# Attention plus two expert layers on one core: order of weight loads and splits, width of the filler's products, and which engine makes the first unit's sums

## The chip, the cores and the metric

The kernel runs on one core of one Trainium2 chip. The metric is the device time of one execution in microseconds (us). The median of three runs before the change is 2114.24 us, from 2111.54 to 2114.75. The trace that is read here is of a fourth execution, the profiled one, which took 2118.01 us; its span from the first to the last instruction is 2116.2 us.

## The reference

Three layers follow one another, all in float32.

```python
# 1. attention: 4 batches x 8 heads, 512 local and 32 global tokens, head size 64, window 32
out_g = softmax(q_g @ [k_g, k_l]^T / 8) @ [v_g, v_l]
out_l = softmax([q_l @ k_g^T / 8, masked(q_l @ k_l^T / 8)]) @ [v_g, v_l]
x = rows of both, 2176 x 512
# 2. eight experts, mixed by Sinkhorn weights
P = exp(x @ w_gate - max)
8 times: P /= P.sum(1); P /= P.sum(0); P *= N / E
x = sum over e of P[:, e] * (relu(x @ w1[e]) @ w2[e])        # 512 -> 1024 -> 512
# 3. one wide layer
x = elu(x @ w_in) @ w_out                                    # 512 -> 2048 -> 512
```

The weights of the last layer come as float64 and are made into float32 pairs by the kernel.

## The kernel before

Every float32 operand of a large product is kept as a rounded high part ("h") and a rest ("l"), and a product is three matmuls, hh, hl and lh (`three`, L107 to L114; L853 to L855). The high part is a cast on ScalarE (ACT), the rest a subtraction on VectorE (DVE) or GpSimd (POOL). All DMAs go through the one queue of SyncE (SP). Each engine works its own instructions off in the order of the program, which is written out by hand (`manual_schedule`).

The stages, with the times of the profiled execution:

- **Attention, about 0 to 262 us** (L470 to L590). TensorE gets filler between the pieces of attention: `filler` (L460) runs half-experts 0 and 1 ("units" u) on the 1024 tokens of the first part by `unit_plain` (L413). That one treats a block of 512 tokens as two halves of 256 columns: four PSUM tiles of the first product (`mm1`), each of 12 matmuls of 256 columns, then two tiles of the second product (`mm2_part`) of 12 matmuls of 512 columns each. Every matmul is one step of the generator; `fill_for(200)` takes steps worth about 200 ns. `swap` loads and splits unit 1's weights beside it, at counted steps.
- **Transition, about 262 to 350 us** (L941 to L959). What is left of the filler runs as a loop. Every 4th step takes one entry of `pre`, every 8th one of `plan`. `pre` holds the sums of blocks of x (`sums_of_x`, L617: `whole` adds high and rest, `comb` adds or subtracts two blocks, `hi` and `lo` split the result), two loads, and the start of unit 2's weights (`weights1`, L663). `plan` is the Sinkhorn iteration (`sinkhorn`, L760): `rows` on DVE, then a matmul (`pcs`, L794) that waits for `rows`, then `cols` on DVE. What is left of `plan` is laid between the products of the first unit.
- **Units on the first part of the tokens (p = 0), units 2 to 15, about 303 to 884 us, and on the second part (p = 1), units 0 to 15, about 884 to 1728 us** (loop at L960). A unit is `mix1` and then `mix2_all`. `mix1` makes the first product in a seven-product scheme: 13 products of six matmuls of 512 columns for p = 0, 27 products of six matmuls of 288 columns for p = 1. Each product ends in PSUM and is taken out by ACT (s, L834) and DVE (u, L836; t, L822); ACT then makes hh (L825) from t, and DVE the rest hl (L827) from t and hh. There are eight PSUM banks and three buffers of t. After each product one entry of the list `side1` is issued. `mix2_all` makes eight or nine second products of twelve matmuls of 512 columns; after each, four entries of `side2` are issued.
- **The wide layer, about 1728 us to the end** (L1043 on), which the change doesn't touch.

What stands in the two lists before the change: `side1` is the four splits of this unit's second weights (`nbuild`; `split`, L99: cast L101 on ACT, subtraction L105 on POOL), then the two loads of the next unit's first weights (`ld1`, L669), then the loads of float64 pieces (L728). `side2` is the building of the next unit's first weights (`b1`, 18 entries), then the conversion of one or two float64 pieces (`weights64`, L720: `words` is six DVE instructions, `parts` two ACT and three POOL instructions and two stores to scratch, L755 and L756, each waiting on SP for what it stores), then the two loads of the next unit's second weights (`ld2`, L714). Raw weights, float64 pieces and block sums share four buffers (`raw_tile`). Units 20 to 25 of the list `order`, counted from 0, convert two pieces, the other units one; the first two and the last before the change of part convert none.

Of the kernel before, what the change touches and what calls it, by code (L numbers as in the profile page):

```python
# [16 lines left out]
ALU = mybir.AluOpType  # L17
# [31 lines left out]
def tile_net(ctx: ExitStack, tc, kq, vw, vc, qg, wg, w1, w2, wi, wo, consts, out):  # L49
# [362 lines left out]

    def unit_plain(u, b, swap=None):  # L413

        for c0 in (0, 256):
            leave, come = (swap is not None and u == v and c0 == 256 * (1 - v) for v in (0, 1))
            hh, hl = (hs[p][:, :, c0:c0 + 256] for p in "hl")
            if leave:
                next(swap)
                next(swap)  # L420
            n = 0
            for r in mm1(wA, lambda p, k: xcols(p, k, b)[:, c0:c0 + 256], 256, hh, hl):
                yield r
                n += 1
                if come and n % 12 == 0:
                    next(swap, None)
            n = 0
            for o in (0, 128):
                i = b * 4 + (c0 + o) // 128
                ps = psm.tile([128, 512], F32, tag="m", name="m2")  # L430
                for r in mm2_part(wA, ps, hh, hl, o, range(4)):
                    yield r
                    n += 1
                    if leave and n % 6 == 0:
                        next(swap)
                if u == 0:
                    nc.vector.tensor_copy(accs[i], ps)
                else:
                    nc.vector.tensor_tensor(out=accs[i], in0=ps, in1=accs[i], op=ALU.add)
                yield "q"  # L440

    rawp = att.enter_context(tc.tile_pool(name="rawp", bufs=3, side="left"))

# [173 lines left out]
    def sums_of_x(p, m):  # L617

        v = {}

        def blk(n, q):
            return xop[n + q][:, :, :m]

        def whole(n, src, eng):
            v[n] = raw_tile((2, m), F32, "x" + n)
            eng.tensor_tensor(out=v[n], in0=blk(src, "h").bitcast(F32), in1=blk(src, "l").bitcast(F32), op=ALU.add)

        def comb(dst, a, b, op, buf):
            nc.vector.tensor_tensor(out=v[buf], in0=v[a], in1=v[b], op=op)
            v[dst] = v[buf]  # L630

        def hi(n):
            nc.scalar.copy(blk(n, "h"), v[n])

        def lo(n):
            nc.vector.tensor_tensor(out=blk(n, "l"), in0=v[n], in1=blk(n, "h").bitcast(F32), op=ALU.subtract)

        load = [
            lambda n=n, q=q, k=k, i=i: nc.sync.dma_start(
                xop[n + q][:, :, :m].bitcast(F32), xd[q][:, 2 * k:2 * k + 2, i * m:(i + 1) * m]  # L640
            )
            for n, i, k in (("s4", 1, 0), ("22", 1, 1), ("11", 0, 0), ("12", 0, 1)) for q in "hl"
        ] if p else []
        return load, [
            lambda: whole("21", "s4", nc.gpsimd),
            lambda: whole("22", "22", nc.vector),
            lambda: comb("s1", "21", "22", ALU.add, "22"),
            lambda: hi("s1"),
            lambda: whole("11", "11", nc.gpsimd),
            lambda: lo("s1"),  # L650
            lambda: comb("s3", "11", "21", ALU.subtract, "21"),
            lambda: comb("s2", "s1", "11", ALU.subtract, "22"),
            lambda: hi("s2"),
            lambda: hi("s3"),
            lambda: lo("s2"),
            lambda: lo("s3"),
            lambda: whole("12", "12", nc.vector),
            lambda: comb("s4", "12", "s2", ALU.subtract, "12"),
            lambda: hi("s4"),
            lambda: lo("s4"),  # L660
        ]

    def weights1(u):  # L663

        v = {}

# [15 lines left out]

        def lo(n):
            src = v[n] if n[0] == "t" else blk(n)
            nc.vector.tensor_tensor(out=wop[n + "l"], in0=src, in1=wop[n + "h"].bitcast(F32), op=ALU.subtract)  # L685

        g, sub = nc.gpsimd, ALU.subtract
        return [lambda: load(0), lambda: load(1)], [
# [71 lines left out]
    def sinkhorn():  # L760
# [31 lines left out]
        def cols():  # L792
            ps = ps2.tile([128, 512], F32, tag="n", name="pcs")
            nc.tensor.matmul(ps[:, :E], ones, s["c"], start=True, stop=True)  # L794
            r = sm.tile([128, E], F32, tag="rc", name="rc")
            nc.vector.tensor_scalar_add(r, ps[:, :E], 1e-9)
            nc.vector.reciprocal(r, r)
            nc.vector.tensor_tensor(
                out=pr, in0=pr, in1=r.rearrange("p (o e) -> p o e", o=1).to_broadcast([128, NT, E]), op=ALU.mult
            )  # L800
            nc.vector.tensor_scalar_mul(pr, pr, float(T) / E)

        return [gmax, None, expm] + [rows, None, cols] * 8

# [136 lines left out]
    with tc.manual_schedule():  # L941
        conv = deque(range(8 * U2))
        plan, sums = sinkhorn(), sums_of_x(0, SL)[1]
        first, build = weights1(2)

        pre, plan = deque(sums[:-2] + first + build[:9]), deque(plan)
        steps = 0
        for r in fill:
            steps += 1
            if steps % 4 == 0:  # L950
                pop(pre)
            if steps % 8 == 0:
                pop(plan)
        pop(pre, len(pre))
        for f in build[9:13]:
# [4 lines left out]
        for a, (p, u) in enumerate(order):  # L960
            after = order[a + 1] if a + 1 < len(order) else None
            switch = after is not None and after[0] != p
            if a > 0:
                side1.extendleft(reversed(nbuild))
            else:
                side1.extend(nbuild)
            cv = []
            if after is not None:
                ld1, b1 = weights1(after[1])
                ld2, nbuild = weights2(after[1])  # L970
                side1.extend(ld1)
                if not switch:
                    for _ in range(min(len(conv), 0 if a < 2 else 2 if 19 < a < 26 else 1)):
                        cv.append(weights64(conv.popleft()))
                    side1.extend(ld for ld, _ in cv)
            if a == 0:

                rest, n = list(side1), len(plan)
                side1.clear()
                for b in range(n):  # L980
                    side1.extend(rest[b * len(rest) // n:(b + 1) * len(rest) // n])
                    side1.append(plan.popleft())
            last = mix1(p, u)
            pop(side1, len(side1))
            if after is None:
                break
            if switch:
                ldx, sums = sums_of_x(1, HALF)

                for f in ldx[4:]:  # L990
                    f()
                b1 = ldx[:4] + [f for pair in zip(b1, sums[:12]) for f in pair] + b1[12:] + sums[12:14]
                nbuild = sums[14:] + nbuild
            side2.extend(b1)
            for _, ops in cv:
                side2.extend(ops)
            side2.extend(ld2)
            mix2_all(p, u, last)
            pop(side2, len(side2))
            if switch:  # L1000
                for i in range(TP[0] // 128):
                    nc.sync.dma_start(yd[:, i], accs[i])
# [176 lines left out]
```

## Time and profile before

| what | value |
|---|---|
| median of three runs | 2114.24 us |
| the three runs | 2114.24, 2114.75, 2111.54 us |
| profiled execution: its time, its span | 2118.01 us, 2116.2 us |
| mean granted TensorE clock | 0.979 |
| busy share of the span: PE, PEld, DVE, ACT, POOL | 96, 84, 64, 35, 34 % |

PE is TensorE with its matmuls, PEld the loading of weights into it. Matmuls are pipelined, so a busy PE is not a PE at its peak; its idle time is real. In timelines the first number is the start of an instruction in us from the start of the span, the second its length, x2 says that two like it follow one another, and in brackets stand the idle time of the engine ahead of it and what ended that. In rows of windows the columns are the stretch, its length, busy time of PE, PEld, DVE, ACT and POOL (with the count of instructions), the granted clock of TensorE as a share of full speed, the busy share of the DMA engines and their GB/s.

### The profile page before, as it was taken

What the parts mean: (1) busy time and instruction counts of PE and PEld (TensorE: products, weight loads), DVE (VectorE), ACT (ScalarE), POOL (GpSimd) and SP (SyncE); (2) the same over time, 40 slices, a digit from 0 to 9 for tenths busy, and PEclk for the clock granted to TensorE, in tenths of its full rate; (3) what the DMA queues carried; (4) which work ended last, traced back from release to release, by engine and by line L of the source; (5) the groups of instructions that cost most, each with busy time, mean ns of one, the idle gap of its engine ahead of it and who ended that gap; (6) DMA issues with size and microseconds to landing.
All of it is one profiled execution on the core that took longest, in us unless ns stands there. A gap on an engine that the chain in (4) does not pass through costs nothing.

```text
span 2116.2 us, 29201 instructions
## 1 busy us (share of the span) xinstructions
PE 2026.4 (96%) x11115; PEld 1768.1 (84%) x11115; DVE 1362.9 (64%) x2534; ACT 747.0 (35%) x1488; POOL 710.1 (34%) x605
## 2 busy tenths in 40 slices
PE   9999979999999999899999988888999999999999
PEld 8998968888888888788888877787888888888897
DVE  7666586676776776766666666666666654444454
ACT  6555424323333332233333322222233333343343
POOL 6545313233333433323322233333332211222222
PEclk9999999999999999999999999999999999999999
DMA  7435221123112211422211222222221140202001
GB/s 229 136 121 175 70 91 60 30 65 114 61 60 97 83 60 68 149 100 82 70 61 60 71 80 80 79 71 71 70 76 64 51 179 1 80 1 80 1 31 55
DMA packets 56444, 168.45 MB, mean 80 GB/s; under 512 B 6128, under 2 KB 7920, under 8 KB 54256
## 3 DMA queue, kind: packets, MB, share of 16 engines
q1 hardware_dynamic: 56304, 166.59, 23.5%
q8 instruction: 87, 1.43, 0.3%
q14 instruction: 53, 0.43, 0.1%
HBM read 138.52 MB, written 28.05 MB: 79 GB/s over the span
## 4 chain that ended last, share of the span: by engine, by line
PE 73%; DVE 10%; ACT 5%; issue 5%; DMA 4%; POOL 2%; SPq 0%; DVEq 0%; ACTq 0%; POOLq 0%
PE m L113 13%; PE m L109 13%; PE m L111 13%; PE q L853 8%; PE q L855 7%; PE q L854 7%; DMA w2r<-in_w_dram 3%; PE o L310 2%; DVE hl L827 2%; DVE eg L130 2%; PE m L1088 1%; PE m L1087 1%; PE m L1090 1%; ACT w2h L101 1%; PE ptp L293 1%
## 5 line engine op out<-in xcount | busy, mean ns | idle before, releaser
L113 PE MATMUL m<-w2h,hl 128*128 128x512 f32 x1088 | 427.0, 392 | 0.0
L109 PE MATMUL m<-w2h,hh 128*128 128x512 f32 x1088 | 426.9, 392 | 0.0
L111 PE MATMUL m<-w2l,hh 128*128 128x512 f32 x1088 | 426.9, 392 | 0.0
L827 DVE SCALAR_TENSOR_TENSOR hl<-t,hh 128x288 fp32r<-128x288 f32 (+1 forms) x368 | 262.9, 714 | 108.5 <-ACT hh L825 103.6
L825 ACT ACTIVATE hh<-t 128x288 fp32r<-128x288 f32 (+1 forms) x368 | 182.1, 500 | 347.8 <-DVE t L822 347.8
L891 DVE SCALAR_TENSOR_TENSOR acc<-m,pr,acc 128x512 f32<-128x512 f32 x247 | 184.3, 749 | 179.6 <-PE m L113 177.9
L105 POOL TENSOR_TENSOR w2l<-w2r,w2h 128x512 fp32r<-128x512 f32 x120 | 171.3, 1457 | 202.2 <-ACT w2h L101 202.2
L113 PEld LDWEIGHTS m<-w2h,hl 128*128 128x128 f32 x1088 | 204.3, 188 | 41.4
L111 PEld LDWEIGHTS m<-w2l,hh 128*128 128x128 f32 x1088 | 204.4, 188 | 40.6
L109 PEld LDWEIGHTS m<-w2h,hh 128*128 128x128 f32 x1088 | 204.4, 188 | 40.1
L822 DVE TENSOR_TENSOR t<-q,u 128x288 f32<-128x288 f32 (+1 forms) x276 | 144.9, 525 | 62.2 <-PE q L855 55.1
L677 POOL TENSOR_TENSOR wt<-w1r 128x512 f32<-128x512 f32 x60 | 78.6, 1311 | 300.1 <-DVE hl L827 251.0
L130 DVE SCALAR_TENSOR_TENSOR eg<-eg,er 128x384 f32<-128x384 f32 (+1 forms) x80 | 77.1, 964 | 148.8 <-ACT er L129 148.8
L677 POOL TENSOR_TENSOR wt<-w1r,wt 128x512 f32<-128x512 f32 x60 | 87.9, 1465 | 234.1 <-DVE wl L685 113.7
L136 POOL TENSOR_SCALAR hh<-eg 128x384 fp32r<-128x384 f32 (+1 forms) x60 | 33.5, 558 | 311.6 <-DVE eg L131 310.5
L681 ACT CAST wh<-wt 128x512 fp32r<-128x512 f32 x120 | 68.8, 619 | 171.4 <-POOL wt L677 171.4
L101 ACT CAST w2h<-w2r 128x512 fp32r<-128x512 f32 x120 | 68.1, 614 | 157.9 <-DMA w2r<-in_w_dram 157.9
L752 POOL TENSOR_TENSOR cp<-r,cp 128x512 f32<-128x512 f32 x32 | 42.0, 1312 | 204.6 <-ACT r L751 204.6
L127 ACT ACTIVATE er<-m 128x384 f32<-128x384 f32 (+1 forms) x80 | 42.8, 535 | 192.0 <-PE m L113 128.3
L853 PE MATMUL q<-x11h,wh 128*128 128x288 f32 (+1 forms) x184 | 62.8, 341 | 34.7 <-DVE t L822 34.7
L685 DVE TENSOR_TENSOR wl<-wt,wh 128x512 fp32r<-128x512 f32 x120 | 88.8, 758 | 0.0
L836 DVE TENSOR_TENSOR u<-q,s 128x288 f32<-128x288 f32 (+1 forms) x92 | 48.4, 526 | 55.0 <-PE q L855 44.0
(268 smaller groups left out, 5066.0 us busy)
## 6 DMA issues: line engine op xcount, KB each, us to landing
w1r<-in_w_dram SPq DMA_DIRECT2D x60, 512.0 KB, 6.7
w2r<-in_w_dram SPq DMA_DIRECT2D x60, 512.0 KB, 5.1
kq<-in_kq_dram SPq DMA_DIRECT2D x31, 544.0 KB, 3.9
r<-in_wi_dram SPq DMA_DIRECT2D x16, 512.0 KB, 4.0
r<-in_wo_dram SPq DMA_DIRECT2D x16, 512.0 KB, 4.0
vw<-in_vw_dram SPq DMA_DIRECT2D x32, 227.5 KB, 4.7
vc<-in_vc_dram SPq DMA_DIRECT2D x8, 568.8 KB, 4.6
raw<-in_w_dram SPq DMA_DIRECT2D x16, 256.0 KB, 5.4
```

Source lines behind the costliest of these rows:

```text
L105: e.tensor_tensor(out=lo, in0=src, in1=hi.bitcast(F32), op=ALU.subtract)
L109: nc.tensor.matmul(ps, ah, bh, start=first, stop=False)
L111: nc.tensor.matmul(ps, ah, bl, start=False, stop=False)
L113: nc.tensor.matmul(ps, al, bh, start=False, stop=last)
L677: eng.tensor_tensor(out=t, in0=get(a), in1=get(b), op=op)
L822: nc.vector.tensor_tensor(out=t, in0=ps, in1=rest, op=ALU.add)
L825: nc.scalar.activation(hh, t, AF.Relu)
L827: late.append(lambda: nc.vector.scalar_tensor_tensor(out=hl, in0=t, scalar=0.0, in1=hh.bitcast(F32), op0=ALU.max, op1=ALU.subtract))
L853: nc.tensor.matmul(ps, wh, xh, start=k == 0 and i != 3, stop=False, skip_group_check=True)
L854: nc.tensor.matmul(ps, wh, xl, start=False, stop=False, skip_group_check=True)
L855: nc.tensor.matmul(ps, wl, xh, start=False, stop=k == 1, skip_group_check=True)
L891: nc.vector.scalar_tensor_tensor(out=accs[i], in0=ps, scalar=scale, in1=accs[i], op0=ALU.mult, op1=ALU.add)
```

## The change

Four things are changed.

- `unit_plain` treats 512 columns at once: `mm1` has matmuls of 512 columns, then four tiles of `mm2_part` follow. The steps at which `swap` is advanced, and the rate at which the loop of the transition takes from `pre` and `plan` (every 3rd and 6th step), are adapted to the halved count of steps of `mm1`.
- For p = 0 the sums 22 and 12 and the rests of s1 and s2 (`sums_of_x`), and all seven rests of unit 2's first weights (`weights1`), are made on GpSimd and no longer on VectorE.
- In `cols` the two multiplications are one instruction.
- `side1` now begins with `ld1`; then come 8 empty entries (p = 1) or 3 (p = 0), then the four splits, then the float64 loads. In `side2`, `ld2` comes ahead of the conversions. At the change of part the last two sums stand at the front of `side1`.

```diff
     def unit_plain(u, b, swap=None):
-        for c0 in (0, 256):
-            leave, come = (swap is not None and u == v and c0 == 256 * (1 - v) for v in (0, 1))
-            hh, hl = (hs[p][:, :, c0:c0 + 256] for p in "hl")
+        leave, come = (swap is not None and u == v for v in (0, 1))
+        hh, hl = (hs[p][:, :, :SL] for p in "hl")
...
-            for r in mm1(wA, lambda p, k: xcols(p, k, b)[:, c0:c0 + 256], 256, hh, hl):
+        for r in mm1(wA, lambda p, k: xcols(p, k, b), SL, hh, hl):
...
-            for o in (0, 128):
+        for o in range(0, SL, 128):
...
-        def lo(n):
-            nc.vector.tensor_tensor(out=blk(n, "l"), in0=v[n], in1=blk(n, "h").bitcast(F32), op=ALU.subtract)
+        def lo(n, eng=nc.vector):
+            eng.tensor_tensor(out=blk(n, "l"), in0=v[n], in1=blk(n, "h").bitcast(F32), op=ALU.subtract)
+        eng = nc.vector if p else nc.gpsimd
...
-            lambda: whole("22", "22", nc.vector),
+            lambda: whole("22", "22", eng),
...
-            lambda: lo("s1"),
+            lambda: lo("s1", eng),
...
-            lambda: lo("s2"),
+            lambda: lo("s2", eng),
...
-            lambda: whole("12", "12", nc.vector),
+            lambda: whole("12", "12", eng),
...
-    def weights1(u):
+    def weights1(u, eng=nc.vector):
...
-            nc.vector.tensor_tensor(out=pr, in0=pr, in1=r..., op=ALU.mult)
-            nc.vector.tensor_scalar_mul(pr, pr, float(T) / E)
+            nc.vector.scalar_tensor_tensor(out=pr, in0=pr, scalar=float(T) / E, in1=r..., op0=ALU.mult, op1=ALU.mult)
...
-        first, build = weights1(2)
+        first, build = weights1(2, nc.gpsimd)
...
-            if steps % 4 == 0:
+            if steps % 3 == 0:
                 pop(pre)
-            if steps % 8 == 0:
+            if steps % 6 == 0:
                 pop(plan)
...
-            if a > 0:
-                side1.extendleft(reversed(nbuild))
-            else:
-                side1.extend(nbuild)
             cv = []
             if after is not None:
                 ld1, b1 = weights1(after[1])
+                side1.extend(ld1)
+            side1.extend([None] * ((8 if p else 3) if a > 0 else 0) + nbuild)
+            if after is not None:
                 ld2, nbuild = weights2(after[1])
-                side1.extend(ld1)
...
-                nbuild = sums[14:] + nbuild
-            side2.extend(b1)
+                side1.extend(sums[14:])
+            side2.extend(b1 + ld2)
             for _, ops in cv:
                 side2.extend(ops)
-            side2.extend(ld2)
```

## Rows read from the trace of the kernel before

**Rows 1.** Windows by stage: the transition's loop; then the last lines of two answers, which sum 13 whole units of p = 0 (351.89 to 884.58 us) and 14 whole units of p = 1 (945.27 to 1673.86 us); then the first and the last unit of p = 1, the last with the start of what follows it. A sum line has no clock.

```profile
262.00:303.00 41.00, 31.21 (x178) 27.01 (x177) 30.53 (x66) 9.78 (x19) 6.63 (x4) 0.88 0.33 115
...
sum 532.69, PE 532.69 PEld 439.23 DVE 368.51 ACT 166.16 POOL 192.88; mean PE 40.98 PEld 33.79 DVE 28.35 ACT 12.78 POOL 14.84
...
sum 728.59, PE 676.35 PEld 611.50 DVE 484.62 ACT 220.50 POOL 234.66; mean PE 48.31 PEld 43.68 DVE 34.62 ACT 15.75 POOL 16.76
...
884.58:945.27 60.69, 52.50 (x278) 46.91 (x276) 48.78 (x79) 21.31 (x41) 16.17 (x12) 0.89 0.25 83
...
1673.86:1728.00 54.14, 51.98 (x308) 47.16 (x307) 30.00 (x57) 14.57 (x32) 7.23 (x6) 0.97 0.34 122
```

**Rows 2.** Windows of three single units of p = 1: two behind a unit that converts one float64 piece, one behind a unit that converts two.

```profile
945.27:994.12 48.85, 47.05 (x278) 42.56 (x277) 32.38 (x62) 15.29 (x33) 15.02 (x12) 1.00 0.19 66
994.12:1044.59 50.47, 48.57 (x278) 44.08 (x277) 32.69 (x62) 15.37 (x33) 15.04 (x12) 0.97 0.19 63
...
1297.37:1352.97 55.60, 48.96 (x277) 44.24 (x276) 37.58 (x69) 16.34 (x35) 19.10 (x15) 0.94 0.23 76
```

**Rows 3.** Who waited for whom, over the whole span: from the list of PE and from the list of ACT (total us, times, longest us).

```profile
PE q L853 <- DVE t L822: 53.8, 21, 6.0
...
ACT w2h L101 <- DMA w2r<-in_w_dram: 157.9, 28, 9.3
```

**Rows 4.** Timelines around the start of the unit at 1297.37 us, behind a unit with two pieces, from the answers for DVE, SP, ACT, DVE again and PE.

```profile
1300.64 1.41 DVE L891 SCALAR_TENSOR_TENSOR acc<-m,pr,acc 128x512 f32<-128x512 f32 x2
...
1305.60 0.32 SPq L756 DMA_DIRECT2D wd2l<-cl  x1
1306.02 0.87 SPq L714 DMA_DIRECT2D w2r<-in_w_dram  x2
...
1311.13 1.14 ACT L101 CAST w2h<-w2r 128x512 fp32r<-128x512 f32 x2 [9.30 <-DMA w2r<-in_w_dram]
...
1312.64 0.76 DVE L827 SCALAR_TENSOR_TENSOR hl<-t,hh 128x288 fp32r<-128x288 f32 x1 [8.94 <-ACT hh L825]
...
1307.52 0.29 PE L855 MATMUL q<-x22h,wl 128*128 128x288 f32 x1
1313.83 0.61 PE L853 MATMUL q<-x11h,wh 128*128 128x288 f32 x1 [6.01 <-DVE t L822]
```

**Rows 5.** Timelines of SP and ACT around the start of the unit at 1093.38 us, behind a unit with one piece.

```profile
1095.41 0.88 SPq L714 DMA_DIRECT2D w2r<-in_w_dram  x2
...
1100.42 1.14 ACT L101 CAST w2h<-w2r 128x512 fp32r<-128x512 f32 x2 [5.60 <-DMA w2r<-in_w_dram]
```

**Rows 6.** Timelines of DVE and POOL in the same two-piece unit: the end of the building of first weights, the same DVE instruction of the conversion in a first and a second piece, DVE's rests hl beside and behind POOL's work.

```profile
1290.09 0.68 DVE L685 TENSOR_TENSOR wl<-w1r,wh 128x512 fp32r<-128x512 f32 x1
...
1291.74 0.43 DVE L739 TENSOR_SCALAR ct<-ct 128x512 f32<-128x512 f32 x1
...
1295.19 1.48 DVE L739 TENSOR_SCALAR ct<-ct 128x512 f32<-128x512 f32 x1
...
1295.08 1.31 POOL L752 TENSOR_TENSOR cp<-r,cp 128x512 f32<-128x512 f32 x1 [7.70 <-ACT r L751]
...
1311.83 5.63 POOL L105 TENSOR_TENSOR w2l<-w2r,w2h 128x512 fp32r<-128x512 f32 x4 [6.25 <-ACT w2h L101]
...
1316.61 1.16 DVE L827 SCALAR_TENSOR_TENSOR hl<-t,hh 128x288 fp32r<-128x288 f32 x1
...
1318.62 0.45 DVE L827 SCALAR_TENSOR_TENSOR hl<-t,hh 128x288 fp32r<-128x288 f32 x1
```

**Rows 7.** Prices of what is moved or joined: the block sums of L626 on POOL and on DVE and the rests of first weights, as minimum, median and maximum in ns, first and last start; then the second multiplication of `cols` from the groups by form in the first 352 us (busy us, mean ns, idle).

```profile
L626 POOL TENSOR_TENSOR x<-xs4h,xs4l x2: 2387/2526/2666, 259.4 to 872.8; 128x1024 f32<-128x1024 f32 x1, 128x1152 f32<-128x1152 f32 x1
...
L626 DVE TENSOR_TENSOR x<-x12h,x12l x2: 1212/1277/1342, 285.4 to 896.8; 128x1024 f32<-128x1024 f32 x1, 128x1152 f32<-128x1152 f32 x1
...
L685 DVE TENSOR_TENSOR wl<-wt,wh x120: 673/682/1773, 297.6 to 1667.2; 128x512 fp32r<-128x512 f32 x120
...
L801 DVE TENSOR_SCALAR pr<-pr 128x136 f32<-128x136 f32 x8 | 2.9, 368 | 0.3
```

**Rows 8.** The transition: the three long idle times of PE from its timeline, and the window behind the first of them.

```profile
290.90 0.59 PE L794 MATMUL pcs<-cs,ones 128*128 128x8 f32 x2 [7.11 <-DVE cs L789]
...
311.01 0.39 PE L794 MATMUL pcs<-cs,ones 128*128 128x8 f32 x2 [2.00 <-DVE cs L789]
...
316.93 0.39 PE L794 MATMUL pcs<-cs,ones 128*128 128x8 f32 x2 [2.65 <-DVE cs L789]
...
290.90:296.90 6.00, 6.00 (x28) 6.00 (x29) 4.79 (x16) 1.78 (x4) 0.00 (x0) 0.50 0.25 88
```

**Rows 9.** The same kind of rest at the change of part, on DVE beside a POOL instruction: timelines of DVE and of POOL.

```profile
880.68 3.35 DVE L636 TENSOR_TENSOR xs1l<-x,xs1h 128x1152 fp32r<-128x1152 f32 x1
...
880.13 2.68 POOL L626 TENSOR_TENSOR x<-x11h,x11l 128x1152 f32<-128x1152 f32 x1 [3.41 <-issue]
```

**Rows 10.** Filler between pieces of attention, PE's timeline: one step of 512 columns and the piece behind it, then two steps of 256 columns and the piece behind them.

```profile
100.29 0.47 PE L113 MATMUL m<-w2h,hl 128*128 128x512 f32 x1
100.60 0.56 PE L310 MATMUL o<-vw,pt 112*128 112x65 f32 x4
...
101.99 0.36 PE L109 MATMUL m<-x11h,wh 128*128 128x256 f32 x1
...
102.31 0.56 PE L310 MATMUL o<-vw,pt 112*128 112x65 f32 x4
```

More of the change, by code (lines that the diff above doesn't have):

```diff
@@ L413, in unit_plain @@
     def unit_plain(u, b, swap=None):
-        for c0 in (0, 256):
-            leave, come = (swap is not None and u == v and c0 == 256 * (1 - v) for v in (0, 1))
-            hh, hl = (hs[p][:, :, c0:c0 + 256] for p in "hl")
[L418 to L421, printed above, removed]
-            for r in mm1(wA, lambda p, k: xcols(p, k, b)[:, c0:c0 + 256], 256, hh, hl):
+        leave, come = (swap is not None and u == v for v in (0, 1))
+        hh, hl = (hs[p][:, :, :SL] for p in "hl")
+        if leave:
+            next(swap)
+            next(swap)
+        n = 0
+        for r in mm1(wA, lambda p, k: xcols(p, k, b), SL, hh, hl):
+            yield r
+            n += 1
+            if come and n % 12 == 0:
+                next(swap, None)
+        n = 0
+        for o in range(0, SL, 128):
+            i = (b * SL + o) // 128
+            ps = psm.tile([128, 512], F32, tag="m", name="m2")
+            for r in mm2_part(wA, ps, hh, hl, o, range(4)):
                 yield r
                 n += 1
-                if come and n % 12 == 0:
-                    next(swap, None)
-            n = 0
-            for o in (0, 128):
[L429 to L437, printed above, removed]
-                else:
-                    nc.vector.tensor_tensor(out=accs[i], in0=ps, in1=accs[i], op=ALU.add)
-                yield "q"
+                if leave and n % 12 == 0:
+                    next(swap)
+            if u == 0:
+                nc.vector.tensor_copy(accs[i], ps)
+            else:
+                nc.vector.tensor_tensor(out=accs[i], in0=ps, in1=accs[i], op=ALU.add)
+            yield "q"
     rawp = att.enter_context(tc.tile_pool(name="rawp", bufs=3, side="left"))
@@ L684, in lo @@
             src = v[n] if n[0] == "t" else blk(n)
-            nc.vector.tensor_tensor(out=wop[n + "l"], in0=src, in1=wop[n + "h"].bitcast(F32), op=ALU.subtract)
+            eng.tensor_tensor(out=wop[n + "l"], in0=src, in1=wop[n + "h"].bitcast(F32), op=ALU.subtract)
         g, sub = nc.gpsimd, ALU.subtract
@@ L797, in cols @@
             nc.vector.reciprocal(r, r)
[L798 to L799 removed]
+            nc.vector.scalar_tensor_tensor(
+                out=pr, in0=pr, scalar=float(T) / E, in1=r.rearrange("p (o e) -> p o e", o=1).to_broadcast([128, NT, E]),
+                op0=ALU.mult, op1=ALU.mult,
             )
[L801 removed]
         return [gmax, None, expm] + [rows, None, cols] * 8
```

1 line of the change is left out of this document (removed).

## The prediction

> **What bounds the kernel now.** I read the windows by stage first, because the average share of PE hides that the stages differ. In the 13 whole units of p = 0 PE is busy for the whole 532.69 us: 40.98 us a unit, no idle time, nothing to win [rows 1]. In the 14 whole units of p = 1 it is busy for 676.35 of 728.59 us, and in the transition's loop for 31.21 of 41.00 us [rows 1]. So the change can only pay in p = 1 and in the transition. The wide layer it leaves alone.
>
> Next, single units of p = 1. The first in [rows 2] takes 48.85 us, with PE busy for 47.05 at full clock: 47.05 is what a unit costs without a stall. The second has 1.90 us of idle time, but is busy 1.5 us longer: its granted clock is 0.97, which is to say that for a while after the stall the clock was the lower of its two levels, 1.2 instead of 2.4 GHz. The third has 6.64 us of idle time and a clock of 0.94, and takes 55.60 us, 8.55 more than it needs.
>
> Then the waits. PE waited 53.8 us in 21 places for t of DVE, and ACT waited 157.9 us in 28 places for the landing of w2r [rows 3]. The timelines join the two [rows 4]. SP can issue the w2r load only behind the store of the second converted piece, which waits for POOL (1305.60), so it goes out at 1306.02. The first split of the second weights is the head of `side1`, so ACT stands in front of it from 1301.83 to 1311.13. Behind it in ACT's order stands hh; DVE waits 8.94 us for hh, all three buffers of t are taken, no PSUM bank comes free, and PE, which ran until 1307.8, stands for 6.01 us. Behind a one-piece unit it is the same with 5.60 us on ACT instead of 9.30 [rows 5], and PE loses 1.7 to 1.9. A p = 0 unit hides the same wait, because eight banks there last twice as long.
>
> **The change part by part.** *Loads and splits of second weights.* With `ld2` ahead of the conversions, SP issues it as soon as buffers are free. In a one-piece unit both buffers come free early in `mix2_all`, and the load lands over 10 us before the next `mix1`. In a two-piece unit the second one needs the buffer that the building of first weights reads last, with the DVE instruction at 1290.09 [rows 6]; issued at about 1290.8 and landing after the 5.0 to 5.1 us from issue to cast of [rows 4, 5], it is there at 1296, ahead of `mix1` (1297.4). The split moreover stands behind ten entries of `side1`, so after the eleventh of `mix1`'s 27 products: a unit's 28 products (the last one stands in `mix2_all`) and nine tiles make 47.05 us, a tile is 2.73 us (12 matmuls of 40.98/180 us), so a product is (47.05 - 24.6)/28 = 0.80 us, and the split comes 8.8 us into `mix1`. The wait on ACT is gone with some 9 us to spare.
>
> What it is worth: 14 units take 728.59 us and need 14 x 47.05 = 658.7; that is 69.9 us. The last unit has 54.14 - 51.98 = 2.16 us of idle time and a clock of 0.97, like the second of [rows 2], so another 3.7 [rows 1]. Together 73.6 us. The first unit of p = 1 takes 60.69 us, 13.6 more than it needs, but its wait is for the sums at the change of part, which stay on DVE: I count 0 there.
>
> What is late next: POOL's four rests take 5.63 us, and beside them DVE's hl takes up to 1.16 instead of 0.45 us [rows 6]. They now fall in the middle of `mix1`. About five hl at +0.5 us make DVE 2.5 us later over a stretch in which it otherwise waits for PE; I estimate 0 to 0.6 us of stall for a unit and take 0. In the six two-piece units the conversions now both start after the sixth tile of `mix2_all`, not after the fifth and the sixth. The first starts 2.7 us later, and the second is slowed beside the first one's POOL part, as it is now (0.43 against 1.48 us, [rows 6]). DVE reaches `mix1`'s first evacuation now at 1300.64 + 1.41 = 1302.05, 4.7 us into it; I expect 4.5 to 6. PE can run on for six products on free banks, 4.8 us, and needs each older bank as DVE reaches it. Bounds: 0, and what a one-piece unit loses now with its clock, 3.4 us. I take 0.5, nearer to the first because the stall of [rows 4] came only when DVE stood still, 10.4 us into `mix1`. That is 3 us for six units, and 6 x 3.4 + 9 x 0.6 = 26 us at the worst. So p = 1 gives 70.6, from 47 to 73.6 us.
>
> The late split has its cover: for p = 0 it starts after 6 products of 6 x 0.228 = 1.37 us, at 8.2 us, its last rest ends at about 12.3 + 2 = 14.3, and `mix1` ends at 17.8 us: 3.5 us of cover. For p = 1 it ends at about 8.8 + 0.6 + 5.6 = 15.0 of 27 x 0.80 = 21.6 us. The `ld1` loads, now at SP's front, wait at most for the conversion's buffer; the float64 loads wait behind the splits, and are read some 30 us later. Both cost 0.
>
> *First unit on GpSimd.* Off DVE: four block sums and rests of 1.21 us and seven rests of 0.68, 9.6 us, and eight times L801, 2.9 us together [rows 7]. On POOL: 4 x 2.39 = 9.6 and 7 x 1.41 (5.63/4, [rows 6]) = 9.9 us, with little else there (6.63 of 41.00 us, [rows 1]). The path is PE waiting for `pcs`, so for DVE: 7.11 us, then 6.00 us at half clock, worth 3.0, and later 2.00 + 2.65 [rows 8]: 14.8 us are to be had. But DVE now waits for POOL in its own order: s1 needs sum 22, s2 is written over s1 and needs its rest done, s4 needs sum 12. And what stays on DVE is slowed beside POOL: 3.35 us for a rest [rows 9] that takes 1.34 at most on a free DVE for the same size [rows 7]. Working through the loop with these prices I find the long stall at some 5 instead of 7.11 us and 1.3 at the first `pcs`; with fewer steps before the first unit one more round of `rows` and `cols` falls into it, where DVE is full, some 2.5 us. Net I take a gain of 2 us, between a gain of 9 and a loss of 8.
>
> The Trainium skill speaks against this move: its GPSIMD Engine Reference, section Engine selection, gives elementwise work on two inputs to VectorE and calls GpSimd about two times slower, and its section Key points says that GpSimd shares its SBUF interfaces with VectorE and contends with instructions of two SBUF inputs. The trace agrees with both: 2.39 against 1.21 us [rows 7], and 3.35 us beside POOL [rows 9]. By that rule the transition would get slower, and that is the third case below.
>
> *Filler.* A step of 512 columns and its gap take 100.60 - 100.29 = 0.31 us, two of 256 take 102.31 - 101.99 = 0.32 [rows 10]. Of 192 such pairs most lie in attention: 192 x 0.01 = 2 us, from 0 to 3; I take 1.5. Each tile of `mm1` is held for twice as long, which I cost at nothing, since PE between pieces of attention always has a next step.
>
> Sum: 70.6 + 2 + 1.5 = 74.1 us. The profiled execution took 2118.0, 3.8 above the median; 2114.2 - 74.1 = 2040 us for the median.
>
> **The rivals.** (1) *The wait moves to DVE.* With ACT free, p = 1 is held by DVE's backlog behind two-piece conversions and by hl beside POOL. For it: hl at 1.16 and a conversion step at 1.48 us [rows 6]. Against: DVE is busy for 484.62 of 728.59 us [rows 1]. p = 1 then gives 47 instead of 70.6: 2064 us. (2) *The change doesn't do what it says in two-piece units*: the second w2r load still comes too late or the buffers hold it, and these six units keep their 8.4 us: 74 - 50 = 24, so 2090 us. For it: the landing has only 1 us ahead of `mix1`; against: ten entries of delay. (3) *GpSimd becomes the path of the transition*: all of its 19.5 us stand in a row instead of DVE's 9.6, DVE waits in line, and the transition loses 8: 2050 us. For it [rows 9]; against: POOL starts early, its sums need nothing of PE. (4) *Slower:* the second products wait for the late split. Place: the first tile of `mix2_all` in 13 units of p = 0 and 15 of p = 1. It decides when the splits end over 3.5 us late in p = 0 and 6.6 in p = 1, as they would with the 9.30 us wait of [rows 4] still in front of them: 5.8 us in 13 units and 2.7 in 15 are 116 us of new stalls, and with no more than the 74 won, 2156 us. Against: w2r lands ahead of `mix1` in every case worked out above.
>
> **How the numbers follow.** Forecast 0.67, its own range 2028 to 2052; rival 1 0.15, rival 2 0.05, rival 3 0.09, rival 4 0.03; 0.01 for no change that can be told. The likeliest is 2040. The bounds of the forecast's terms give 2114 - 73.6 - 9 - 3 = 2028 at best; for stalls that the lower clock makes longer than I see I go to 2022. Upward the range takes in rivals 3 and 1, so 2067. It leaves out rivals 2 and 4. Faster by over 0.2% (about what a measurement of this kernel tells from no change): all but rival 4 and no change, 0.96; within 0.01; slower 0.03.
>
> **What would show it.** In the changed profile ACT's wait for w2r should be gone from the list, PE's 53.8 us for t should be under 5, all units of p = 1 but the first should take 47 to 48 us at clock 1.00, and those of p = 0 still 40.98. If two-piece units alone are longer, rival 1 (waiting for t, ACT not waiting for a DMA) or 2 (ACT waiting for one) has it. PE waiting for w2l would be rival 4. In the transition `pcs` should still wait, for some 10 us in all; if DVE's x there waits for POOL for long, rival 3. The forecast is wrong if p = 1 units keep over 1 us of idle time each, or if attention's end moves by more than 3 us.

## The result and the profile after

The changed kernel takes 2052.21 us (median of three runs, 2051.05 to 2053.56) against 2114.24 us: a ratio of 0.971, interval 0.9688 to 0.9732. It is 62.0 us faster, where 74.1 were forecast: inside the range given, and 0.2 us above the upper end of the forecast's own (2052). The profiled execution takes 2052.21 us, with a span of 2050.4. Runs here are compared with undisturbed runs only; of one experiment (sixteen entries) the profiled execution was disturbed, so only its times are used.

The wait lists come first, since the prediction named what should go from them. PE's list after (total us, times, longest us):

```profile
PE pcs L795 <- DVE cs L790: 14.9, 5, 6.3
PE q L854 <- DVE t L823: 6.9, 7, 1.8
PE q L854 <- ACT xs2h L632: 4.6, 1, 4.6
```

PE's 53.8 us for t [rows 3] have become 6.9, of which 1.8 lie in the unit at the change of part; the prediction wanted to see under 5. Its waits for `pcs`, 14.9 us, were to be some 10. ACT's 157.9 us for the landing of w2r [rows 3] are no longer in ACT's list. Windows of the changed kernel, in the order of rows 1 and 2: the transition's loop; the first unit; the sums of 13 whole units of p = 0 and of 14 of p = 1 (949.08 to 1612.26 us); then a unit behind one float64 piece and one behind two.

```profile
262.00:302.50 40.50, 29.73 (x125) 22.23 (x123) 27.10 (x41) 9.46 (x15) 24.31 (x14) 0.92 0.33 113
302.58:355.71 53.13, 46.37 (x192) 36.93 (x191) 36.99 (x79) 19.00 (x32) 13.30 (x10) 0.94 0.18 60
...
sum 532.65, PE 532.65 PEld 439.23 DVE 372.76 ACT 167.84 POOL 185.39; mean PE 40.97 PEld 33.79 DVE 28.67 ACT 12.91 POOL 14.26
...
sum 663.18, PE 658.10 PEld 595.89 DVE 500.64 ACT 223.92 POOL 234.41; mean PE 47.01 PEld 42.56 DVE 35.76 ACT 15.99 POOL 16.74
...
949.08:995.88 46.80, 46.80 (x277) 42.53 (x276) 33.18 (x62) 15.56 (x33) 14.72 (x12) 1.00 0.21 68
...
1278.03:1326.16 48.13, 47.29 (x277) 42.61 (x276) 39.19 (x69) 16.56 (x35) 19.44 (x15) 1.00 0.28 88
```

What the reader is to see: p = 0 is as it was (532.65 against 532.69 us [rows 1]). A one-piece unit has no idle time left and a granted clock of 1.00 (46.80 us, from 48.85 and 50.47 [rows 2]). A two-piece unit keeps 0.84 us of idle time and takes 48.13 us, from 55.60 [rows 2]. The first unit is longer: the same window of the kernel before reads

```profile
303.10:351.92 48.82, 44.17 (x189) 35.67 (x188) 37.60 (x76) 19.00 (x32) 12.40 (x9) 0.97 0.21 65
```

So the account by the starts of stages in the two traces is: the first unit starts 0.5 us earlier (302.58 against 303.10) and is 4.3 longer, so 3.8 us are lost; p = 0 and the unit at the change of part (60.7 us in both) change nothing; the 14 whole units of p = 1 give 728.59 - 663.18 = 65.4 us, and the last unit 3.9 more; the wide layer begins 65.5 us earlier, and the span ends 65.8 us earlier.

That the 14 units gained so much is in part the luck of one execution. The kernel with the old lists and everything else changed ("the rest alone" below) has the same 14 units in 6.0 us less than before, and all its one-piece units at a clock of 1.00:

```profile
sum 722.58, PE 672.04 PEld 607.14 DVE 483.90 ACT 220.36 POOL 234.47; mean PE 48.00 PEld 43.37 DVE 34.56 ACT 15.74 POOL 16.75
```

In the profiled execution of before, three of its eight one-piece units had 0.97 and took 50.5 to 50.7 us, the others 48.7 to 49.4.

The stall that is left in the two-piece units, from the timelines of DVE, POOL and PE in the unit at 1278.03 us:

```profile
1277.50 1.53 DVE L742 TENSOR_SCALAR cp<-r 128x512 int32<-128x512 int32 x1
1279.07 1.66 DVE L743 TENSOR_TENSOR ct<-ct,cp 128x512 int32<-128x512 int32 x1
1280.77 1.40 DVE L744 TENSOR_SCALAR cp<-ct 128x512 int32<-128x512 int32 x1
...
1283.41 0.44 DVE L837 TENSOR_TENSOR u<-q,s 128x288 f32<-128x288 f32 x1
...
1290.56 1.45 DVE L828 SCALAR_TENSOR_TENSOR hl<-t,hh 128x288 fp32r<-128x288 f32 x1
1291.93 0.45 DVE L823 TENSOR_TENSOR t<-q,u 128x288 f32<-128x288 f32 x1
1292.30 1.18 DVE L828 SCALAR_TENSOR_TENSOR hl<-t,hh 128x288 fp32r<-128x288 f32 x1
...
1295.34 1.19 DVE L828 SCALAR_TENSOR_TENSOR hl<-t,hh 128x288 fp32r<-128x288 f32 x1
...
1278.71 1.47 POOL L754 TENSOR_TENSOR ct<-ct,ch 128x512 f32<-128x512 f32 x1
...
1290.40 2.77 POOL L105 TENSOR_TENSOR w2l<-w2r,w2h 128x512 fp32r<-128x512 f32 x2 [4.16 <-ACT w2h L101]
1293.44 2.77 POOL L105 TENSOR_TENSOR w2l<-w2r,w2h 128x512 fp32r<-128x512 f32 x2 [0.27 <-ACT w2h L101]
...
1297.51 0.40 PE L854 MATMUL q<-xs4h,wh 128*128 128x288 f32 x1 [0.84 <-DVE t L823]
```

DVE reaches the unit's first evacuation at 1283.41, 5.4 us in, since the second conversion's last three instructions take 1.40 to 1.66 us beside POOL. Before it has caught up, POOL's rests of the second weights make its hl slow, 1.18 to 1.45 us. PE stands only after both, ahead of 1297.51.

### The profile page after: what moved, and what is told of

It reads as the page before. It is cut to its first block, busy times and chain, and to the rows that moved or that the text cites. A ratio compares the mean times of both kernels' runs of the same rounds, so it can differ in the third digit from the quotient of the medians.

```text
span 2050.4 us, 28802 instructions
## 1 busy us (share of the span) xinstructions
PE 2004.9 (98%) x10923; PEld 1735.3 (85%) x10923; DVE 1378.3 (67%) x2499; ACT 750.3 (37%) x1472; POOL 720.4 (35%) x616
## 5 line engine op out<-in xcount | busy, mean ns | idle before, releaser
L828 DVE SCALAR_TENSOR_TENSOR hl<-t,hh 128x288 fp32r<-128x288 f32 (+1 forms) x368 | 286.3, 778 | 3.9 <-ACT hh L826 0.5
L105 POOL TENSOR_TENSOR w2l<-w2r,w2h 128x512 fp32r<-128x512 f32 x120 | 160.6, 1354 | 240.4 <-ACT w2h L101 224.4
L750 ACT CAST ch<-ct 128x512 fp32r<-128x512 f32 x32 | 19.9, 623 | 202.0 <-DVE ct L743 202.0
L310 PEld LDWEIGHTS o<-vw,pt 112*128 112x128 f32 x512 | 73.6, 191 | 7.2 <-ACT pt L298 2.1
```

The lines of the kernel that those rows point to most:

```text
L105: e.tensor_tensor(out=lo, in0=src, in1=hi.bitcast(F32), op=ALU.subtract)
L310: nc.tensor.matmul(s["o"][:, i, :], pt[:, (i % 2) * 2 + j, :], s["v"][:, i, j, :], start=(j == 0), stop=(j == 1))
L828: late.append(lambda: nc.vector.scalar_tensor_tensor(out=hl, in0=t, scalar=0.0, in1=hh.bitcast(F32), op0=ALU.max, op1=ALU.subtract))
```

## The experiments

"List edits" are the new order of `side1` and `side2`; "the rest" is the filler in products of 512 with its two rates, the joined multiplication, and GpSimd's sums and rests. Medians in us; before is that of the same batch.

| run | us (from, to) | before | ratio [interval] |
|---|---|---|---|
| list edits alone | 2047.16 (2045.01, 2048.20) | 2114.14 | 0.9683 [0.9668, 0.9698] |
| `ld2` ahead alone | 2048.82 (2048.10, 2049.45) | 2114.14 | 0.9692 [0.9677, 0.9707] |
| late splits alone | 2051.02 (2049.69, 2052.01) | 2114.14 | 0.9702 [0.9687, 0.9717] |
| the rest alone | 2119.76 (2115.83, 2124.66) | 2114.14 | 1.0034 [1.0019, 1.0049] |
| list edits + filler | 2052.96 (2051.39, 2055.32) | 2113.66 | 0.9712 [0.9698, 0.9727] |
| list edits + GpSimd | 2047.81 (2045.36, 2049.16) | 2113.66 | 0.9686 [0.9671, 0.9700] |
| list edits + joined | 2046.24 (2045.88, 2046.84) | 2113.66 | 0.9680 [0.9665, 0.9694] |
| list edits + spread | 2038.16 (2035.90, 2040.17) | 2113.66 | 0.9639 [0.9622, 0.9655] |
| filler, 16 entries | 2045.35, 2045.35, 2049.02, 2050.27 | 2112.34 | 0.9692 [0.9672, 0.9712] |
| filler, 18 entries | 2049.39 (2047.34, 2050.73) | 2112.34 | 0.9702 [0.9687, 0.9718] |
| 14 empty entries | 2040.75 (2039.33, 2044.30) | 2112.34 | 0.9665 [0.9648, 0.9681] |
| all but the filler, spread | 2037.88 (2035.92, 2040.61) | 2113.59 | 0.9646 [0.9630, 0.9662] |

### The lists, together and by halves

List edits alone are the kernel before with the last part of the change's diff, from `if a > 0:` on. "Late splits" is its half in `side1`: first-weight loads ahead, the empty entries, and only then the splits. "`ld2` ahead" is its half in `side2`: the second-weight loads ahead of the conversions.

> The kernel before with the two lists alone reordered (first-weight loads ahead, splits after 8 or 3 empty entries, second-weight loads ahead of the conversions); filler, GpSimd and Sinkhorn as before. My theory: all of the gain of the units of p = 1 is here. The units from the second of p = 1 to the last should take 663 us in place of 728.6, the two-piece ones with 0.85 us of idle time each, the first unit should start at 303.1 and the second at 351.9 us as before, and the whole should take 69 us less than before, about 2045 us, which is some 4 us less than the changed kernel beside its own profile. The rival, that the other edits carry part of it, expects under 60 us.

> The kernel before with one edit: the loads of second weights ahead of the float64 conversions; the splits stay at the head of the list. Theory A, the wait is the landing: the load lands ahead of the first product (by over 10 us behind a one-piece unit, by 1 us behind a two-piece one), ACT's 157.9 us of waiting for it go to under 15, and at least 60 of the 69 us come. Theory B, the splits have to leave the head of the list because they fill ACT and POOL there: under 25 us come, and the units of p = 1 keep 1 us or more of idle time each.

> The kernel before with the other half: first-weight loads ahead and the splits after 8 or 3 empty entries, the loads of second weights still behind the conversions. By the rows of before, such a load lands 7 us into the first products behind a one-piece unit and 14 us behind a two-piece one, and the first split is then due 8.8 us in. Theory A: one-piece units run free (47.1 us), two-piece units keep ACT waiting for some 5 us in the middle and lose 1 to 3 us each; 50 to 65 us come in all. Theory B expects 60 us or more with two-piece units free as well.

> The changed kernel with the two lists put back: 512-column filler, the first unit's sums and rests on GpSimd, the joined multiplication. By the two traces: the first unit starts 0.5 us earlier and the second 3.8 us later than before; units of p = 1 keep their stalls, so the whole takes 0 to 8 us more than before (2114 to 2122). The rival, that the lists cost the first unit its 4 us, expects the second unit at 352 us or earlier.

The list edits alone give 2047.16 us, 67.0 less than before (69 were expected from two profiled executions), and the rest alone makes the kernel slower by 0.34%; its second unit starts at 356.8 us, 4.9 later than before, so it is not the lists that the first unit loses by. So the whole gain is the lists', and the rest takes some 5 us of it back. With the rest alone ACT's wait stays as it was:

```profile
ACT w2h L101 <- DMA w2r<-in_w_dram: 156.6, 28, 9.5
```

By halves, `ld2` ahead gives nearly all of the gain by itself (65.3 us by the medians, of 67.0), and so do late splits (63.1): a one-piece unit takes 46.81 us with either. The halves are not parts of a sum. Theory A holds for both: late splits alone bring 63.1 of its 50 to 65 us, and their two-piece units are not free, as Theory B would have them. The two times are not told apart, the intervals overlap; by the traces they differ in two-piece units alone, which take 48.1 to 48.2 us with `ld2` ahead and 48.0 to 49.2 with late splits. The list of ACT with late splits alone still has

```profile
ACT w2h L101 <- DMA w2r<-in_w_dram: 18.7, 6, 3.7
```

six waits, one for each two-piece unit, with 10.6 us for t in PE's list (6.9 after). A two-piece unit with `ld2` ahead alone reads

```profile
1275.00:1323.15 48.15, 47.25 (x278) 42.58 (x277) 38.63 (x69) 16.48 (x35) 19.78 (x15) 1.00 0.27 88
```

and ACT's list there has no wait for w2r at all, so its 0.9 us of idle time has another cause.

### The parts of the rest

The edits are those hunks of the change, each added to the list edits.

> The kernel with the reordered lists alone, plus the 512-column filler with its rates of every 3rd and 6th step. Theory A, the loss of the first stage is GpSimd's: this one is like the lists alone, 2047 us within 2, with the second unit within 2 us of 351. Theory B, the loss is the filler's, because fewer steps leave more rounds of the Sinkhorn iteration to the first unit, where VectorE is full: 3 to 6 us more than the lists alone, the second unit at 354 us or later.

> The lists alone, plus the four sums and rests and the seven weight rests of the first unit on GpSimd; filler and joined multiplication as before. Theory A: VectorE waits for GpSimd in its own order and is slowed beside it; 3 to 6 us more than the lists alone (2050 to 2053), the second unit at 354 us or later. Theory B: 2047 us within 2, or less.

> The lists alone, plus the joined multiplication. Eight instructions of 0.23 us less on VectorE, on the chain of the Sinkhorn rounds: 1 to 2 us less than the lists alone (2045 to 2046). The rival, that the joined one takes as long as the two, expects 2047.

The filler costs 5.8 us by the medians, so Theory B of its run holds. GpSimd's part is not told from nothing (0.9686 against 0.9683), and the joined multiplication neither (0.9680). The traces say the same of GpSimd. Sums of the stretch from the last matmul of the logits to the start of the second unit, with list edits alone (265.13 to 350.36 us), with GpSimd's part added (266.14 to 350.91) and with the filler added (267.23 to 356.85):

```profile
sum 85.23, PE 71.43 PEld 59.50 DVE 64.84 ACT 28.24 POOL 17.28; mean PE 35.71 PEld 29.75 DVE 32.42 ACT 14.12 POOL 8.64
```

```profile
sum 84.77, PE 69.99 PEld 57.89 DVE 67.11 ACT 28.09 POOL 34.20; mean PE 35.00 PEld 28.94 DVE 33.55 ACT 14.05 POOL 17.10
```

```profile
sum 89.62, PE 74.24 PEld 57.41 DVE 66.55 ACT 27.86 POOL 16.62; mean PE 37.12 PEld 28.70 DVE 33.27 ACT 13.93 POOL 8.31
```

With 11 instructions moved away, DVE is busy for no less time, 67.11 us against 64.84. What GpSimd's part takes in the loop it gives back in the first unit: PE's long stall grows from 7.11 to 8.84 us, and the unit takes 47.16 us, with 3.01 of idle time, instead of 50.27 with 4.68.

```profile
291.65 0.59 PE L796 MATMUL pcs<-cs,ones 128*128 128x8 f32 x2 [8.84 <-DVE cs L791]
```

The price on DVE is seen in one rest that stays on DVE, xs3l: first with list edits alone, then with GpSimd's part added and with the POOL instructions beside it.

```profile
279.79 1.22 DVE L636 TENSOR_TENSOR xs3l<-x,xs3h 128x1024 fp32r<-128x1024 f32 x1
```

```profile
280.10 2.58 DVE L636 TENSOR_TENSOR xs3l<-x,xs3h 128x1024 fp32r<-128x1024 f32 x1
...
279.19 2.40 POOL L636 TENSOR_TENSOR xs2l<-x,xs2h 128x1024 fp32r<-128x1024 f32 x1 [3.38 <-ACT xs2h L633]
281.55 3.32 POOL L626 TENSOR_TENSOR x<-x12h,x12l 128x1024 f32<-128x1024 f32 x1
```

DVE is rid of xs2l, and pays 1.36 us more for xs3l. Where the filler loses is seen in PE's timeline: its starts of the column sums `pcs`, a pair of matmuls a round, with list edits alone

```profile
278.20 0.39 PE L794 MATMUL pcs<-cs,ones 128*128 128x8 f32 x2 [0.96 <-DVE cs L789]
288.54 0.59 PE L794 MATMUL pcs<-cs,ones 128*128 128x8 f32 x2 [7.11 <-DVE cs L789]
293.54 0.28 PE L794 MATMUL pcs<-cs,ones 128*128 128x8 f32 x2
298.25 0.28 PE L794 MATMUL pcs<-cs,ones 128*128 128x8 f32 x2
302.86 0.28 PE L794 MATMUL pcs<-cs,ones 128*128 128x8 f32 x2
```

and with the filler added

```profile
283.45 0.39 PE L793 MATMUL pcs<-cs,ones 128*128 128x8 f32 x2 [1.89 <-DVE cs L788]
293.21 0.39 PE L793 MATMUL pcs<-cs,ones 128*128 128x8 f32 x2 [3.78 <-DVE cs L788]
299.04 0.28 PE L793 MATMUL pcs<-cs,ones 128*128 128x8 f32 x2
305.04 0.60 PE L793 MATMUL pcs<-cs,ones 128*128 128x8 f32 x2 [2.22 <-DVE cs L788]
...
327.57 0.39 PE L793 MATMUL pcs<-cs,ones 128*128 128x8 f32 x2 [2.53 <-DVE cs L788]
```

The first unit starts at 300.09 and at 299.50: four rounds lie ahead of it in the one, three in the other. The filler has 74 steps instead of 128, and every sixth of 74 takes 12 entries of the balancing schedule, where every eighth of 128 took 16; so a round more falls into the first unit. Its windows, first with list edits alone, then with the filler added:

```profile
300.09:350.36 50.27, 45.59 (x190) 36.78 (x188) 35.98 (x76) 19.04 (x32) 12.39 (x9) 0.93 0.20 63
```

```profile
299.50:356.85 57.35, 49.45 (x192) 38.70 (x191) 41.88 (x90) 19.09 (x32) 12.35 (x9) 0.88 0.18 55
```

The unit is 7.1 us longer: idle time grows by 3.2 us (from 4.68 to 7.90), and PE is busy 3.9 longer at a lower granted clock, 0.88 instead of 0.93. How much of the second part is chance is open: the first unit of the kernel before, shown above, has the same 4.65 us of idle time, a clock of 0.97 and 48.82 us. Two runs ask whether giving the entries back mends it:

```diff
-            if steps % 6 == 0:
+            if steps % 9 in (0, 4):      # 16 entries;  steps % 4 == 0 for 18
                 pop(plan)
```

> Both list edits and the filler in products of 512, but the balancing schedule's entries taken 16 times in the filler's 74 steps, as often as the kernel before takes them in its 128 (the changed kernel takes 12). Theory A (the filler's loss is the one round of the balancing loop that twelve entries leave over: it falls into the first mix unit, which is 57.4 us long with it and 50.3 us without): the first unit is back to some 50 us and the kernel to that of the list edits, 2047 us, within 2. Theory B (the products of 512 cost of themselves, by what they wait for inside the filler): 2053 us as with the slower rate, and the loss moves ahead of the first unit.

> As the run before, with an entry at every fourth step: 18 in the filler, a round more than in the kernel before. Theory A (each round taken into the filler is hidden there, and the first unit gets shorter by it): 2042 to 2045 us, first unit 46 us or less. Theory B (the filler cannot hide a further round: a round takes VectorE as long there, and the sum over all ones then waits on TensorE inside the loop): 2047 to 2050 us, with longer waits for the column sums ahead of the first unit.

With 16 entries the ratio is 0.9692, against 0.9712 with 12 and 0.9683 without the filler's change. That speaks for Theory A, but its interval overlaps both, and no trace of it is used. With 18 entries Theory B holds: five rounds lie ahead of the first unit and three in it, the loop waits for `cs` in four places, and the unit is no shorter than the 50.27 us above:

```profile
303.48:354.59 51.11, 44.78 (x187) 35.70 (x186) 37.92 (x72) 19.02 (x32) 12.28 (x9) 0.93 0.19 62
```

The filler can't hide a fifth round. That the missing fourth costs about 4 us is thus supported by times and counts, not shown by a trace with the round put back; that products of 512 columns cost something of themselves is not ruled out.

### The stall of the two-piece units

The spread takes the list edits and moves the conversions, which followed one another behind the sixth tile, apart:

```diff
+            if len(cv) == 2:
+                (w0, p0), (w1_, p1) = (ops for _, ops in cv)
+                side2.extend(b1[:10] + [w0] + b1[10:14] + [p0] + b1[14:] + ld2 + [w1_, p1])
```

> The lists alone, with the two conversions of a two-piece unit spread over the third to sixth tile of the second products in place of all in the sixth. Theory A, the 0.85 us stall of two-piece units is VectorE's backlog from the conversions: it goes, these six units take 46.8 in place of 48.1 us, the whole 8 us less than the lists alone (2039). Theory B, it is VectorE slowed beside GpSimd's four late rests, whatever came before: the stall stays within 0.2 us.

Theory A holds, with 9 us against list edits alone by the medians. The two-piece unit at 1272.05 us, by the window, and DVE's timeline there:

```profile
1272.05:1318.86 46.81, 46.81 (x278) 42.55 (x276) 39.13 (x69) 16.55 (x35) 19.95 (x14) 1.00 0.29 91
```

```profile
1272.50 0.43 DVE L743 TENSOR_SCALAR cp<-ct 128x512 int32<-128x512 int32 x1
1272.85 1.40 DVE L891 SCALAR_TENSOR_TENSOR acc<-m,pr,acc 128x512 f32<-128x512 f32 x2
1274.17 0.45 DVE L836 TENSOR_TENSOR u<-q,s 128x288 f32<-128x288 f32 x1
```

DVE does the same work (39.13 us), but reaches the first evacuation 2.1 us into the unit and not 5.4, and PE never waits.

The other run lets the splits slide further, and asks how much room there is ahead of the second products (the prediction's fourth rival):

```diff
-            side1.extend([None] * ((8 if p else 3) if a > 0 else 0) + nbuild)
+            side1.extend([None] * ((14 if p else 3) if a > 0 else 0) + nbuild)
```

> Both list edits with fourteen empty entries in place of eight ahead of the layer-two split in the second-stage units, so that the four splits fall six products, some 7 us, later. It asks how far the split may slide. Theory A (the room is what the trace of the list edits shows between the last rest on GpSimd and the next matmul that reads any low part, 6.25 us in the one-piece units and 4.85 in the others): the second products wait some 0.9 us in nine units and 2.3 in six, 22 us in all, so 2069 us. Theory B (the last of the four low parts is read only as the fourth product of a tile, so the room is some 2 us more): 2047 to 2050 us.

Neither theory had this: 2040.75 us, where list edits alone gave 2047.16. The intervals of the two ratios overlap, so it is the trace that shows the gain: each of the six two-piece units takes 47.0 us instead of 48.1 and has no idle time. The room was enough, as Theory B has it, and the stall went as well. A two-piece unit and, in it, POOL's rests, DVE's hl beside them, and the first matmul that reads a rest:

```profile
1271.46:1318.48 47.02, 47.02 (x277) 42.58 (x276) 39.11 (x69) 16.48 (x35) 19.63 (x15) 1.00 0.29 90
```

```profile
1288.22 5.71 POOL L105 TENSOR_TENSOR w2l<-w2r,w2h 128x512 fp32r<-128x512 f32 x4 [8.54 <-ACT w2h L101]
...
1288.36 1.47 DVE L827 SCALAR_TENSOR_TENSOR hl<-t,hh 128x288 fp32r<-128x288 f32 x1
...
1285.59 0.46 DVE L836 TENSOR_TENSOR u<-q,s 128x288 f32<-128x288 f32 x1 [0.43 <-ACT s L834]
...
1293.38 0.40 PE L111 MATMUL m<-w2l,hh 128*128 128x512 f32 x1
```

The hl beside POOL are as slow as after (1.47 us), so the contention has not gone. But DVE already waits for its next input at 1285.59, 2.6 us before the rests begin: its backlog from the conversions is worked off when the contention comes. ACT's casts, which slid with the rests, are no third delay: in the stalled unit ACT waits for t ahead of nearly every hh. So the stall was the sum of two delays, each of which PE's free banks can take alone. The second products read their first rest at 1293.38 while POOL is still making the last (to 1293.93); they read the four one after the other, so there is no wait.

### All but the filler, with the spread

The changed kernel with its filler and rates as before, and the spread.

> The changed kernel with its filler and its two rates put back as in the kernel before, and the two conversions of the two-piece units spread over tiles of the second products. Theory A (the filler is the only part of the change that costs, and the stall of the two-piece units goes with the spread, so the parts add): the list edits' 2047 us less 9 for the spread, less up to 1 for the joined multiplication, GpSimd's sums at nothing: 2036 to 2039 us, all second-stage units at 46.8. Theory B (GpSimd's sums and rests cost too, once the joined multiplication stands beside them, as the changed kernel's longer first unit suggests): 2041 to 2044 us, the first unit over 51 us.

Theory A: 2037.88 us, not told apart from the spread on list edits alone. The first unit, with GpSimd's sums and the joined multiplication, takes 46.30 us:

```profile
301.11:347.41 46.30, 44.13 (x189) 35.52 (x188) 34.75 (x68) 18.91 (x32) 13.76 (x10) 0.96 0.21 69
```

So those two parts cost nothing. Both versions with the spread beat the changed kernel, by some 14 us.

## Why the prediction came out as it did

**Second-stage units (p = 1): right in cause and size.** 70.6 us were forecast, 69.3 came. By the profiled executions, that is; the low clock in three one-piece units of the one before is in this number. Two terms inside were each a little off and largely cancelled: a unit without a stall takes 46.81 us and not 47.05, which is 3.4 us in 14 units; the two-piece stall costs 48.1 - 46.8 = 1.3 us in each of six, 8 in all, and not 3. The prediction had DVE reach the first evacuation 4.5 to 6 us in (it is 5.4) and took the stall near nothing because POOL's slowing of hl was counted for each unit by itself, at 0. What failed is that the two were priced apart: either run that separates them in time takes the stall away. That is rival 1 (the wait moves to DVE) on the small scale of six units, and it is why PE's wait for t is 6.9 us and not under 5.

**The loads and splits.** The second w2r load of a two-piece unit goes out and lands ahead of `mix1`, as forecast, and with `ld2` ahead alone ACT's wait is gone too: rival 2 fell. The late split's room was forecast as 6.6 us in p = 1; in the changed kernel 6.25 us lie between the last rest and the first matmul that reads one in a one-piece unit, 4.85 in a two-piece one, and the run with fourteen entries slid the splits by 4.4 us in two-piece units (12.4 us into the unit to 16.8) without a wait. Rival 4 fell; the price of going past that room was not measured.

**The transition: the step that failed.** The sum had +2 us here and +1.5 for the filler; the traces have -3.8 for both. The prediction did see that "one more round of `rows` and `cols` falls into" the first unit, and priced it at 2.5 us. With the filler added to list edits the first unit grew by 7.1 us, over half of it by longer busy time at the lower clock, while the loop ahead of it (from the last matmul of the logits) shortened by 2.7: 4.4 us net. The filler's own gain in attention did not show: the logits end at 267.20 to 267.58 us in the four traces with the new filler, and at 264.93 to 267.48 in the nine with the old one. The other half of the step is GpSimd: relieving DVE was to shorten PE's long stall from 7.11 to some 5 us [rows 8], but GpSimd's part alone made it 8.84, and the changed kernel has 6.28. In all PE waited longer for `pcs`, 14.9 us instead of 12.7 and not some 10.

**GpSimd.** The moved instructions cost twice as much on POOL (2.39 against 1.21 us a sum [rows 7]), and slow what stays on DVE (xs3l, 2.58 for 1.22 us). In the changed kernel POOL is busy for 24.31 of the loop's 40.50 us (6.63 of 41.00 before [rows 1]), and still it neither gains nor loses in its run. The Trainium skill (GPSIMD Engine Reference, section Engine selection) gives two-input elementwise work to VectorE; the prices agree with it, but in the runs here the choice made no measurable difference: the work left VectorE, on which PE was waiting, and VectorE paid about as much back beside POOL. Rival 3 had the transition lose 8 us; it lost 3.8, and by the runs of the parts the filler did it, not GpSimd.

**The rest of the miss.** The traces give 2118.01 - 2052.21 = 65.8 us; 8.3 of the miss of 12 are in the terms above (1.3 in p = 1, 7.3 in the transition and the filler, less 0.3 at the end). The other 3.8 are the distance of the profiled execution of before from its median: the forecast carried it over, but the changed kernel's profiled execution lay on its median. The 6.0 us by which the 14 units of p = 1 differ between two executions with the same lists show where such a distance can come from. So the time came out within the range although the transition's account had the wrong sign.

## What to carry to other kernels

A load that waits at the head of an in-order queue blocks what is queued behind it; issue it earlier or put the consumer later; here either alone gave nearly all (65.3 and 63.1 of 67.0 us). When a schedule is paced by steps of other work, a change of the step size changes how much is left over: count the entries before and after, and price what is left where it lands, with the clock that a row of stalls costs. A small stall behind two delays can go when the delays are moved apart in time, as both did here at the price of reordering a list. And a gain that is read from one trace holds the clock of that one execution: look at a second one before it goes into a sum.

## What the runs showed of the hardware

- A DVE instruction whose operands all lie in SBUF, and that starts while a POOL instruction runs, ends behind it by nearly its whole time alone: by 0.28 us for a conversion step of 0.43 with one input [rows 6], by 1.09 for xs3l of 1.22, by 1.22 for a rest of at most 1.34 [rows 9, 7]. It looks as if it did its work only when POOL had ended, so what it pays depends on how early in POOL's instruction it starts: hl took 1.16 to 1.47 us in the rows shown, instead of 0.45. POOL waits in its turn: its sum behind that xs3l took 3.32 us instead of 2.39 [rows 7]. One that reads PSUM is not slowed: t takes 0.45 us at 1291.93, within POOL's work from 1290.40 to 1293.17. The Trainium skill (GPSIMD Engine Reference, section Key points) names instructions with two SBUF inputs, and those in a two-port mode, as the ones that contend; the trace agrees for hl, and no run here shows in which mode the steps with one input ran.
- An idle time of 0.84 us left the granted clock of the unit at 1.00; before, 1.90 us left it at 0.97 and 6.64 at 0.94 [rows 2]. But another one-piece unit of the kernel before, the row below, had 2.10 us of idle time and 1.00, and the first unit had 0.97 with 4.65 us before and 0.93 with 4.68 with list edits alone.

```profile
1192.54:1241.94 49.40, 47.30 (x277) 42.58 (x276) 33.27 (x64) 15.38 (x33) 14.85 (x12) 1.00 0.23 75
```
